# Attention in units of 512 tokens of one sequence and one pair of heads, before a soft mixture of experts

## The chip, the cores and the metric

The kernel runs on one core of one Trainium2 chip, as one launch. The metric is the device time of the launch in microseconds (us), the median of several runs; lower is better. TensorE is called PE, VectorE DVE, ScalarE ACT, GpSimd POOL; SP is the queue of SyncE, from which this kernel issues all its DMAs (transfers between the chip's memory and the core's).

## What is computed

Inputs are q, k and v of shape (8 sequences, 8 heads, 576 tokens, 64), the matrix phi (512 x 32) and the weights w1 (8 experts, 512 x 1024) and w2 (8 experts, 1024 x 512), all float32. First comes attention within chunks of 64 tokens, then a soft mixture of experts over all 4608 tokens with 512 features:

```python
scores = scale * np.matmul(q_c, k_c.transpose(0, 1, 2, 4, 3))   # chunks of 64 tokens, scale = 1/8
scores = scores - np.max(scores, axis=-1, keepdims=True)
attn = np.exp(scores)
attn = attn / (np.sum(attn, axis=-1, keepdims=True) + 1e-09)
out = np.matmul(attn, v_c)
...
logits = x @ phi                       # x: (4608, 512), heads side by side
d = softmax(logits, over tokens);  slot_input = d.T @ x
slot_out[e] = np.maximum(slot_input[e] @ w1[e], 0.0) @ w2[e]     # 4 slots for each of 8 experts
c = softmax(logits, over slots);   return c @ slot_out
```

(The two softmaxes are abridged here; both subtract the maximum and divide by the sum plus 1e-9.)

## The kernel before, in words

**Stages.** The first stage is attention together with the logits, the running maximum and sum over tokens and the running product `d.T @ x`. It goes over 36 units (`NT`). When the last unit is done, the 32 slot inputs are known, and the second stage runs the experts (`up`, `turn`, `down`) and the final product `c @ slot_out` (`combine`), with output transfers at its end.

**A unit before.** The 4608 tokens are taken as one row of 18 groups of 256 tokens (`GT`), regardless of where a sequence ends; a unit is one group and four of the eight heads (`t = 2 g + z`). Since a sequence has 576 tokens, some groups lie across a boundary, and `pieces` (line 127) splits their transfers. `load_qk` (line 136) brings k and q of a unit to SBUF with two tokens of a head in one row of 512 B; `load_v` (line 146) brings v for one tile of 128 tokens with all eight heads, in rows of 256 B. There are eight buffers for q and k (two per unit, so four units deep) and six for v.

**Steps of a unit.** `transposes(t)` (line 150) turns q and k on PE, eight matmuls against the identity (line 156), and four copies bring the result from PSUM to `qkT` in SBUF, three on ACT (line 165) and one on DVE (line 163), de-interleaving even and odd tokens by writes with a stride of two. `s1` (line 169) computes the scores (line 177), their maximum (185) and the difference (187); `s1b` the exponential on ACT (192). `s2a` transposes the result (201, copy 203); `s2b` multiplies with v (219), where a column of ones beside v gives the sums, and normalises into the tile x (228). `s3` transposes x into `xT` (242, copies 247 and 249). Four tiles of 128 tokens make one batch of 512 tokens: `logits`, `weights`, `natural`, `partial`, `combination` run once per batch, that is once in four units.

**Order.** The schedule is written out by hand: in the loop from line 402 on, iteration t issues the loads (`load_qk(t + 5)`, at even t `load_v(t + 2)` and `load_v(t + 3)`, and the weights w1 at an even pace), then `s1(t)`, `transposes(t + 2)`, `s3(t - 3)`, `s2a(t - 1)`, `s1b(t)`, `s2b(t - 2)`, with the steps of a batch between them. The instructions run on each engine in this order. The last two units and the last two batches are unrolled behind the loop (lines 434 to 474). All loads wait in SP's queue in the order in which they are written; a load whose buffer is still being read holds up those behind it.

**End.** `combine(b, h)` (line 602) computes half of the 512 features for batch b and writes 512 rows of 1 KB (line 617): partition p holds four consecutive tokens.

The functions that the change touches:

Of the kernel before, what the change touches and what calls it, by code (L numbers as in the profile page):

```python
# [16 lines left out]
def kernel(  # L17
# [10 lines left out]
    nc = tc.nc  # L28
# [6 lines left out]
    NC = S // CH  # L35
# [4 lines left out]
    GT = 2 * P  # L40
    HZ = H // 2
# [9 lines left out]
    NV = 6  # L51
    NQK = 8

# [18 lines left out]
    qkn = [qk_w[i // 4][:, 512 * (i % 4):512 * (i % 4 + 1)].rearrange("p (h x) -> p h x", h=HZ)  # L72
# [21 lines left out]
    with ExitStack() as actx:  # L94
# [23 lines left out]
        qkT = tiles("qkT", [3, 2, GT], [0])  # L118
        atb = tiles("at", [4, 2, CH], [0])
        sc2 = ap_.tile([P, 2, DM], F32, name="sc2")  # L120
        xb = tiles("x", [2, DM], range(3))
        xT = ap_.tile([P, 4, NF, P], F32, name="xT")
        v_sb = tiles("v", [H, VW], range(NV))
        qkT.update(tiles("qkT", [3, 2, GT], [1]))
        atb.update(tiles("at", [4, 2, CH], [1]))

        def pieces(t0, n):

            o, t = [], t0
            while t < t0 + n:  # L130
                e = min(t0 + n, (t // S + 1) * S)
                o.append((t - t0, e - t, t // S, t % S))
                t = e
            return o

        def load_qk(u):
            g, z = divmod(u, 2)
            for i, src in enumerate((k, q)):
                dst = qkn[(2 * u + i) % NQK]
                for o, n, b, s0 in pieces(GT * g, GT):  # L140
                    nc.sync.dma_start(
                        dst[o // 2:(o + n) // 2],
                        src[b][HZ * z:HZ * (z + 1), s0:s0 + n].rearrange("h (g j) d -> g h (j d)", j=2),
                    )

        def load_v(t):
            for o, n, b, s0 in pieces(P * t, P):
                nc.sync.dma_start(v_sb[t % NV][o:o + n, :, 0:D], v[b][:, s0:s0 + n].rearrange("h x d -> x h d"))

        def transposes(t):  # L150

            pt = pair(f"pqk_{t}")
            for isq in range(2):
                src = qkn[(2 * t + isq) % NQK]
                for h in range(HZ):
                    nc.tensor.transpose(out=pt[:, 1 - isq, P * h:P * (h + 1)], in_=src[:, h], identity=ident)  # L156
            pv = pt.rearrange("x s (hp a g) -> x a s hp g", hp=2, a=2)
            for j in range(2):
                for a in range(2):
                    r = slice(D * a, D * (a + 1))  # L160
                    o = qkT[t % 2][r, 0:2 + a:1 + a].rearrange("x s hp (g j) -> x j s hp g", j=2)[:, j]
                    if j == 1 and (a == 1 or t == 0):
                        nc.vector.tensor_copy(o, pv[D * j:D * (j + 1), a])  # L163
                    else:
                        nc.scalar.copy(o, pv[D * j:D * (j + 1), a])  # L165
# [3 lines left out]
        def s1(t):  # L169
            psc = bank(f"psc_{t}")  # L170
            qT, kb = qkT[t % 2][:, 0], qkT[t % 2][:, 1:3]

            pv = psc.rearrange("p (s a c x) -> p s c a x", s=2, a=2, c=2)
            for c in range(4):
                cs = slice(CH * c, CH * (c + 1))
                for hp in range(2):
                    nc.tensor.matmul(  # L177
                        pv[CH * hp:CH * (hp + 1), c // 2, c % 2],
                        lhsT=qT[:, hp, cs],
                        rhs=kb[:, :, hp, cs],  # L180
                        start=True, stop=True,
                    )
# [11 lines left out]
        xs = {}  # L194
# [11 lines left out]
        def s2b(t):  # L206
            at = ats.pop(t)
            g, z = divmod(t, 2)
            x = xb[g % 3] if g < NT // 2 - 1 else sc2
            rc = a2.tile([P, 2, 4, 1], F32, tag="rc", name=f"rc_{t}")  # L210
            pav = pair(f"pav_{t}")

            for h in range(4):
                for c2 in range(2):
                    for s in range(2):
                        rs = slice(CH * c2, CH * (c2 + 1))
                        nc.tensor.matmul(  # L219
                            pav[CH * s:CH * (s + 1), c2, h * VW:(h + 1) * VW],  # L220
                            lhsT=at[rs, 2 * s + h % 2, h // 2, :],
                            rhs=v_sb[(2 * g + s) % NV][rs, HZ * z + h, :],
                            start=True, stop=True,
                        )
# [3 lines left out]
            nc.vector.tensor_tensor(  # L228
                x[:, :, HZ * D * z:HZ * D * (z + 1)].rearrange("p c (h d) -> p c h d", d=D),
                av[..., 0:D],  # L230
                rc.to_broadcast([P, 2, 4, D]),
                ALU.mult,
            )
            xs[2 * g], xs[2 * g + 1] = x[:, 0], x[:, 1]

        def s3(t):
            px = bank(f"px_{t}")
            g, z = divmod(t, 2)
            for i in range(2):
                for f in range(2):  # L240
                    fs = slice(P * (2 * z + f), P * (2 * z + f + 1))
                    nc.tensor.transpose(  # L242
                        out=px[:, P * (2 * i + f):P * (2 * i + f + 1)], in_=xs[2 * g + i][:, fs], identity=ident)
            pv = px.rearrange("p (s f x) -> p s f x", s=2, f=2)
# [80 lines left out]
        def partial(b):  # L325
            eN, _, al, _ = lst[b]
            pp = bank(f"pp_{b}")
            for j in range(4):
                nc.tensor.matmul(  # L329
                    pp[SL * j:SL * (j + 1), :],  # L330
                    lhsT=eN[:, j, :],
                    rhs=xs.pop(4 * b + j),
                    start=True, stop=True,
                )
# [46 lines left out]
        for t in v_sb.values():  # L381
            nc.gpsimd.memset(t[:, :, D:VW], 1.0)
        load_v(0)
        load_v(1)
# [56 lines left out]
        s2b(t - 3)  # L441
        s2a(t - 1)
# [159 lines left out]
    def combine(b, h):  # L602
# [4 lines left out]
        for j2 in range(2):  # L607
# [9 lines left out]
        nc.sync.dma_start(  # L617
            out[4 * P * b:4 * P * (b + 1), DH * h:DH * (h + 1)].rearrange("(p j) f -> p j f", j=4), ob)
# [58 lines left out]
```

## Time and profile before

| | |
|---|---|
| median of three timed runs | 262.06 us (261.92 to 262.63) |
| time of the profiled execution | 263.49 us |
| its span (first to last instruction) | 261.6 us |
| busy: PE, DVE, ACT, POOL | 223.2, 168.0, 149.7, 7.2 us |
| moved by DMA | 71.86 MB |
| granted PE clock, mean | 0.969 |

In the page of the profile, one digit stands for one fortieth of the span (6.5 us) and gives the busy share in tenths; "DMA" is the mean busy share of the core's 16 DMA engines, as the time of their packets, so overlapping packets can make it exceed 1 in other views. The attention stage goes to about slice 28, the experts and the output to the end. The list of waits gives, for an engine and line, what ended its idle time, the total in us, how often, and the longest. In the list of DMA issues the last number is the median time from issue to landing.

### The profile page before, as it was taken

The numbers are of one execution on the slowest core, as the hardware profiler recorded it, in microseconds if no ns is written. First come the engines' busy times: TensorE is split into PE (matmuls) and PEld (weight loads), VectorE is DVE, ScalarE is ACT, GpSimd is POOL, SyncE is SP. The second block draws the span as 40 slices with busy tenths as digits, with TensorE's granted clock in tenths as the row PEclk, the third lists the DMA queues.
The fourth block names the chain that finished last, engine by engine and source line by source line (L and its number), as shares of the span: only waits on it lengthen the run. The fifth ranks groups of instructions, "written<-read, shape, count | busy, mean of one in ns | idle before, by whom it ended". The sixth has DMA issues, their size and how long they took to land.

```text
span 261.6 us, 7833 instructions
## 1 busy us (share of the span) xinstructions
PE 223.2 (85%) x3205; PEld 164.9 (63%) x3205; DVE 168.0 (64%) x385; ACT 149.7 (57%) x300; POOL 7.2 (3%) x31
## 2 busy tenths in 40 slices
PE   6988988988897988998797697969899999999840
PEld 3666875775785875775684586657563345776840
DVE  4568786886985986986875855867554020755640
ACT  3597857858758758668657366757221220655530
POOL 1000000000000000000000000000004000000000
PEclk9999999999999999999999979999999999999775
DMA  6999599999999999998998995999999999998797
GB/s 181 259 212 228 150 271 245 291 267 254 309 285 262 318 286 259 244 236 267 234 300 232 175 288 136 305 272 343 348 340 339 351 348 348 349 335 272 255 343 250
DMA packets 106962, 71.86 MB, mean 275 GB/s; under 512 B 40368, under 2 KB 102832, under 8 KB 106928
## 3 DMA queue, kind: packets, MB, share of 16 engines
q1 hardware_dynamic: 106928, 71.38, 101.2%
q8 instruction: 25, 0.41, 0.7%
q14 instruction: 9, 0.07, 0.1%
HBM read 61.93 MB, written 9.44 MB: 273 GB/s over the span
## 4 chain that ended last, share of the span: by engine, by line
PE 42%; DMA 23%; DVE 13%; ACT 13%; issue 3%; SPq 2%; ACTq 0%
DMA qk_w<-in_q_dram 23%; ACT qkT L165 10%; PE pf L610 7%; PE po L575 6%; PE ph L545 5%; PE pqk L156 5%; PE px L242 4%; PE psc L177 3%; DVE qkT L163 3%; PE pav L219 3%; DVE x L228 3%; PE pt L201 2%; DVE xT L247 2%; PE pl L259 2%; PE pp L329 2%
## 5 line engine op out<-in xcount | busy, mean ns | idle before, releaser
L165 ACT COPY qkT<-pqk 64x512 f32<-64x512 f32 x107 | 67.0, 626 | 39.7 <-PE pqk L156 37.9
L156 PE MATMUL pqk<-ident,qk_w 128*128 128x128 f32 x288 | 43.9, 291 | 15.4 <-DMA qk_w<-in_k_dram 6.3
L156 PEld LDWEIGHTS pqk<-ident,qk_w 128*128 128x128 f32 x288 | 31.9, 145 | 27.7 <-DVE qkT L163 8.4
L163 DVE COPY qkT<-pqk 64x512 f32<-64x512 f32 x37 | 25.8, 698 | 32.4 <-ACT qkT L165 29.7
L177 PE MATMUL psc<-qkT 128*64 128x128 f32 x576 | 40.2, 282 | 0.3 <-DVE qkT L163 0.3
L177 PEld LDWEIGHTS psc<-qkT 128*64 128x64 f32 x576 | 31.4, 138 | 3.7 <-issue 1.2
L219 PE MATMUL pav<-v,at 64*64 64x65 f32 x1152 | 25.8, 227 | 0.9 <-issue 0.6
L187 DVE TENSOR_TENSOR sc<-psc,mx 128x512 f32<-128x512 f32 x36 | 24.9, 691 | 1.3
L242 PE MATMUL px<-ident,x 128*128 128x128 f32 x136 | 21.8, 284 | 4.3 <-DVE x L228 4.1
L219 PEld LDWEIGHTS pav<-v,at 64*64 64x64 f32 x1152 | 20.7, 136 | 7.0 <-issue 5.9
L185 DVE TENSOR_REDUCE mx<-psc 128x8 f32<-128x512 f32 x36 | 24.4, 677 | 0.3 <-PE psc L177 0.2
L228 DVE TENSOR_TENSOR x<-pav,rc 128x512 f32<-128x512 f32 x34 | 23.5, 691 | 1.2
L201 PE MATMUL pt<-ident,sc 128*128 128x128 f32 x144 | 22.3, 279 | 1.8 <-ACT sc L192 1.8
L242 PEld LDWEIGHTS px<-ident,x 128*128 128x128 f32 x136 | 15.4, 143 | 12.7 <-DVE x L228 10.9
L192 ACT ACTIVATE sc<-sc 128x512 f32<-128x512 f32 x36 | 23.0, 639 | 0.3 <-DVE sc L187 0.3
L203 ACT COPY at<-pt 128x512 f32<-128x512 f32 x36 | 21.2, 589 | 1.9 <-PE pt L201 1.5
L610 PE MATMUL pf<-sst,cst 128*128 128x256 f32 x72 | 18.7, 413 | 0.9 <-DVE sst L597 0.9
L201 PEld LDWEIGHTS pt<-ident,sc 128*128 128x128 f32 x144 | 17.0, 143 | 2.7 <-ACT sc L192 2.5
L610 PEld LDWEIGHTS pf<-sst,cst 128*128 128x128 f32 x72 | 17.4, 329 | 1.9 <-DVE sst L597 1.3
L616 DVE COPY ob<-pf 128x512 f32<-128x512 f32 x18 | 12.2, 689 | 4.1 <-PE pf L610 4.0
L545 PE MATMUL ph<-w,siT 128*32 128x512 f32 x128 | 14.4, 594 | 0.3 <-DVE s_rd L375 0.3
L614 ACT COPY ob<-pf 128x512 f32<-128x512 f32 x18 | 10.5, 586 | 7.0 <-PE pf L610 6.8
(95 smaller groups left out, 203.4 us busy)
## 6 DMA issues: line engine op xcount, KB each, us to landing
w<-in_moe_w_dram SPq DMA_DIRECT2D x30, 1024.0 KB, 8.4
out_dram<-ob SPq DMA_DIRECT2D x18, 512.0 KB, 5.1
v<-in_v_dram SPq DMA_DIRECT2D x32, 256.0 KB, 6.6
qk_w<-in_k_dram SPq DMA_DIRECT2D x24, 256.0 KB, 6.6
qk_w<-in_q_dram SPq DMA_DIRECT2D x24, 256.0 KB, 6.5
qk_w<-in_moe_w_dram SPq DMA_DIRECT2D x2, 1024.0 KB, 10.3
qk_w<-in_k_dram SPq DMA_DIRECT2D x8, 192.0 KB, 5.7
qk_w<-in_q_dram SPq DMA_DIRECT2D x8, 192.0 KB, 5.8
```

The source lines that it names most:

```text
L156: nc.tensor.transpose(out=pt[:, 1 - isq, P * h:P * (h + 1)], in_=src[:, h], identity=ident)
L163: nc.vector.tensor_copy(o, pv[D * j:D * (j + 1), a])
L165: nc.scalar.copy(o, pv[D * j:D * (j + 1), a])
L177: nc.tensor.matmul(pv[CH * hp:CH * (hp + 1), c // 2, c % 2], lhsT=qT[:, hp, cs], rhs=kb[:, :, hp, cs], start=True, stop=True,)
L185: nc.vector.reduce_max(mx, pv, axis=AX.X)
L187: nc.vector.tensor_tensor(sc.rearrange("p (r x) -> p r x", x=CH), pv, mx.unsqueeze(2).to_broadcast([P, 8, CH]), ALU.subtract)
L201: nc.tensor.transpose(out=pt[:, P * r:P * (r + 1)], in_=sc[:, r], identity=ident)
L219: nc.tensor.matmul(pav[CH * s:CH * (s + 1), c2, h * VW:(h + 1) * VW], lhsT=at[rs, 2 * s + h % 2, h // 2, :], rhs=v_sb[(2 * g + s) % NV][rs ...
L228: nc.vector.tensor_tensor(x[:, :, HZ * D * z:HZ * D * (z + 1)].rearrange("p c (h d) -> p c h d", d=D), av[..., 0:D], rc.to_broadcast([P, 2 ...
L242: nc.tensor.transpose(out=px[:, P * (2 * i + f):P * (2 * i + f + 1)], in_=xs[2 * g + i][:, fs], identity=ident)
L545: nc.tensor.matmul(ph[SL * i:SL * (i + 1), :], lhsT=siT[:, j, :], rhs=wt[1, e, j // 2][:, j % 2, DM * h:DM * (h + 1)], start=(j == 0), sto ...
L610: nc.tensor.matmul(pf[:, DH * j:DH * (j + 1)], lhsT=cv[:, 2 * j2 + j, :], rhs=sst[h], start=True, stop=True)
```

## The change

A unit is now 512 tokens of one sequence (the first 512 of its 576) and a pair of heads; four units (`NHP`) make a batch of 512 tokens with all heads, and there are eight such batches. The last 64 tokens of all eight sequences together are a ninth batch, which is computed fifth. So no load crosses a sequence's end, and `pieces` is gone.

- q and k come with four tokens in a row of 1 KB; each unit has two such loads of 256 KB, or four of 128 KB in the batch of the last tokens. Because four tokens lie side by side, the eight transposes now take two 128-column blocks per head, and the copies of lines 163 and 165 read PSUM alternating between two blocks (`g i`), and write with a stride of two as before.
- v comes per unit, in rows of 256 B as before, in two transfers (one per head), four in the batch of last tokens; it has four buffers, one per unit, and `load_v(t + 1)` is issued in every iteration. `load_v(35)` is issued behind the loop, after `s2b(32)` is written and behind the second load of w2 into `qk_w`.
- `s1`, `s2b`, `s3` and `partial` use other indices; the numbers and shapes of their instructions stay. x has two buffers of a whole batch. `s3` fills one block of 128 features for all four lanes, where it filled two blocks for two lanes.
- Outputs go to their sequence's rows; the batch of the last tokens writes each half in four transfers, one for each of the four consecutive tokens of a partition.

The core of the diff:

```diff
-    GT = 2 * P
-    HZ = H // 2
+    BT = 4 * P
+    RT = S - BT
+    JT = 4
+    GT = RT // JT
-    NV = 6
+    NV = 4
+    batch = [0, 1, 2, 3, B] + list(range(4, B))
...
         def load_qk(u):
-            g, z = divmod(u, 2)
+            n, hp = divmod(u, NHP)
+            hs = slice(2 * hp, 2 * hp + 2)
             for i, src in enumerate((k, q)):
                 dst = qkn[(2 * u + i) % NQK]
-                for o, n, b, s0 in pieces(GT * g, GT):
+                if batch[n] < B:
+                    nc.sync.dma_start(dst, src[batch[n], hs, 0:BT].rearrange("a (g j) d -> g a (j d)", j=JT))
+                else:
+                    for a in range(2):
+                        nc.sync.dma_start(
+                            dst[:, a], src[:, 2 * hp + a, BT:S].rearrange("b (g j) d -> g b (j d)", j=JT))
...
+        def load_v(u):
+            n, hp = divmod(u, NHP)
+            hs = slice(2 * hp, 2 * hp + 2)
+            dst = v_sb[u % NV][..., 0:D]
+            if batch[n] < B:
+                for a in range(2):
                     nc.sync.dma_start(
+                        dst[:, :, a], v[batch[n], 2 * hp + a, 0:BT].rearrange("(r x) d -> x r d", x=P))
+            else:
+                for c2 in range(2):
+                    for a in range(2):
+                        nc.sync.dma_start(dst[CH * c2:CH * (c2 + 1), :, a],
+                                          v[c2::2, 2 * hp + a, BT:S].rearrange("r x d -> x r d"))
...
-            pv = pt.rearrange("x s (hp a g) -> x a s hp g", hp=2, a=2)
+            if batch[u // NHP] < B:
+                pv = pt.rearrange("x s (a i g) -> x a s g i", a=2, i=2)
+                dv = dst.rearrange("x s (g i j) -> x j s g i", i=2, j=2)
+            else:
+                pv = pt.rearrange("x s (a i g b) -> x a s b g i", a=2, i=2, b=B)
+                dv = dst.rearrange("x s (b g i j) -> x j s b g i", b=B, i=2, j=2)
...
-            o = xT[:, 2 * (g % 2):2 * (g % 2) + 2, 2 * z:2 * z + 2]
+            o = xT[:, :, hp]
...
-            if t % 2 == 0:
-                load_v(t + 2)
-                load_v(t + 3)
+            load_v(t + 1)
...
         s2b(t - 3)
+        load_v(t)
         s2a(t - 1)
...
-        nc.sync.dma_start(
-            out[4 * P * b:4 * P * (b + 1), DH * h:DH * (h + 1)].rearrange("(p j) f -> p j f", j=4), ob)
+        ov = out.rearrange("(b s) f -> b s f", s=S)[..., DH * h:DH * (h + 1)]
+        if batch[b] < B:
+            nc.sync.dma_start(ov[batch[b], 0:BT].rearrange("(p j) f -> p j f", j=4), ob)
+        else:
+            for j in range(4):
+                nc.sync.dma_start(ov[:, BT + j:S:4], ob[:, j])
```

More of the change, by code (lines that the diff above doesn't have):

```diff
@@ L34 @@
     CH = 64
-    NC = S // CH
+    NHP = H // 2
     DM = H * D
@@ L71 @@
     qk_w = [const.tile([P, 2048], F32, name=f"qk_w{i}") for i in range(2)]
-    qkn = [qk_w[i // 4][:, 512 * (i % 4):512 * (i % 4 + 1)].rearrange("p (h x) -> p h x", h=HZ)
+    qkn = [qk_w[i // 4][:, 512 * (i % 4):512 * (i % 4 + 1)].rearrange("p (a x) -> p a x", a=2)
            for i in range(NQK)]
@@ L125 @@
+        qkT.update(tiles("qkT", [3, BT], [1]))
         atb.update(tiles("at", [4, 2, CH], [1]))
[L127 to L134, printed above, removed]
         def load_qk(u):
-            g, z = divmod(u, 2)
+            n, hp = divmod(u, NHP)
+            hs = slice(2 * hp, 2 * hp + 2)
             for i, src in enumerate((k, q)):
@@ L139, in load_qk @@
                 dst = qkn[(2 * u + i) % NQK]
-                for o, n, b, s0 in pieces(GT * g, GT):
[L141 to L148, printed above, removed]
@@ new lines, in transposes @@
+        def transposes(u):
+            pt = pair(f"pqk_{u}")
+            for isq in range(2):
+                src = qkn[(2 * u + isq) % NQK]
+                for a in range(2):
+                    for i in range(2):
+                        o = P * (2 * a + i)
+                        nc.tensor.transpose(
+                            out=pt[:, 1 - isq, o:o + P], in_=src[:, a, P * i:P * (i + 1)], identity=ident)
+            dst = qkT[u % 2]
+            if batch[u // NHP] < B:
[4 more added lines that the diff above has]
+                dv = dst.rearrange("x s (b g i j) -> x j s b g i", b=B, i=2, j=2)
@@ L158, in transposes @@
             for j in range(2):
                 for a in range(2):
-                    r = slice(D * a, D * (a + 1))
-                    o = qkT[t % 2][r, 0:2 + a:1 + a].rearrange("x s hp (g j) -> x j s hp g", j=2)[:, j]
-                    if j == 1 and (a == 1 or t == 0):
+                    o = dv[D * a:D * (a + 1), j, 0:2 + a:1 + a]
+                    if j == 1 and (a == 1 or u == 0):
                         nc.vector.tensor_copy(o, pv[D * j:D * (j + 1), a])
@@ L171, in s1 @@
             qT, kb = qkT[t % 2][:, 0], qkT[t % 2][:, 1:3]
[L173 to L182, printed above, removed]
+            pv = psc.rearrange("p (m a c x) -> p m c a x", m=2, a=2, c=2)
+            for c in range(8):
+                m, c2, r2 = c // 4, c // 2 % 2, c % 2
+                o = P * (2 * m + r2) + CH * c2
+                nc.tensor.matmul(
+                    pv[CH * r2:CH * (r2 + 1), m, c2],
+                    lhsT=qT[:, o:o + CH],
+                    rhs=kb[:, :, o:o + CH],
+                    start=True, stop=True,
+                )
             pv = psc.rearrange("p (r x) -> p r x", x=CH)
@@ L233, in s2b @@
             )
-            xs[2 * g], xs[2 * g + 1] = x[:, 0], x[:, 1]
         def s3(t):
             px = bank(f"px_{t}")
[L238 to L244, printed above, removed]
-            o = xT[:, 2 * (g % 2):2 * (g % 2) + 2, 2 * z:2 * z + 2]
+            n, hp = divmod(t, NHP)
+            for j in range(4):
+                nc.tensor.transpose(
+                    out=px[:, P * j:P * (j + 1)], in_=xb[n % 2][:, j % 2, hp, j // 2], identity=ident)
+            pv = px.rearrange("p (j x) -> p j x", j=4)
+            o = xT[:, :, hp]
             if t == NT - 1 or t % 2 == 0 and t < NT - 6:
@@ L381 @@
         for t in v_sb.values():
-            nc.gpsimd.memset(t[:, :, D:VW], 1.0)
+            nc.gpsimd.memset(t[..., D:VW], 1.0)
         load_v(0)
-        load_v(1)
         for t in qkT.values():
```

32 lines of the change are left out of this document (13 added, 19 removed).

## The prediction

> **What bounds the kernel now.** I read the page first, then the list of waits, then windows cut at the starts of every fourth unit, then the DMA view and single rows of SP.
>
> ```profile
> span 261.6 us, 7833 instructions
> ...
> DMA  6999599999999999998998995999999999998797
> GB/s 181 259 212 228 150 271 245 291 267 254 309 285 262 318 286 259 244 236 267 234 300 232 175 288 136 305 272 343 348 340 339 351 348 348 349 335 272 255 343 250
> ...
> PE 42%; DMA 23%; DVE 13%; ACT 13%; issue 3%; SPq 2%; ACTq 0%
> ```
>
> ```profile
> PE pqk L156 <- DMA qk_w<-in_k_dram: 6.3, 8, 1.9
> ...
> PE pqk L156 <- DMA qk_w<-in_q_dram: 1.7, 6, 0.4
> ```
>
> The DMA engines are busy in almost every slice, but they move about 250 GB/s in the first 27 slices (attention) and 348 in the slices behind (weights of the second product). In attention, then, a busy engine moves less. The chain gives 23% to loads of q; that counts each load from its issue, so it tells where the end hangs on transfers, not what would be saved. What would be saved is in the waits: PE sat 6.3 + 1.7 = 8.0 us before line 156, the transposes, with k or q not there. That is the ceiling of what faster loads can give.
>
> The bounds below are starts of line 177 in units 8, 12, ..., 32; each block is four units with the same work (the first and the last of these starts from the PE timeline, then the windows: length, busy time of PE, PEld, DVE, ACT, POOL, granted clock, DMA share, GB/s).
>
> ```profile
> 40.53 1.09 PE L177 MATMUL psc<-qkT 128*64 128x128 f32 x16
> ...
> 163.37 1.09 PE L177 MATMUL psc<-qkT 128*64 128x128 f32 x16
> ```
>
> ```profile
> 40.53:60.20 19.67, 17.34 (x304) 13.74 (x299) 15.55 (x35) 13.74 (x29) 0.40 (x1) 1.00 1.07 268
> 60.20:80.25 20.05, 17.58 (x305) 13.75 (x299) 15.61 (x35) 14.04 (x29) 0.40 (x1) 1.00 1.09 282
> 80.25:99.33 19.08, 17.37 (x304) 13.76 (x298) 15.62 (x35) 14.01 (x29) 0.40 (x1) 1.00 1.16 285
> 99.33:118.72 19.39, 17.83 (x306) 13.86 (x299) 15.61 (x35) 14.02 (x29) 0.40 (x1) 1.00 1.05 239
> 118.72:139.68 20.96, 17.42 (x304) 13.76 (x299) 15.62 (x35) 13.99 (x29) 0.40 (x1) 1.00 1.07 264
> 139.68:163.37 23.69, 18.75 (x305) 15.03 (x299) 15.63 (x35) 14.76 (x30) 0.40 (x1) 0.93 0.89 211
> ```
>
> The third block, 19.08 us, is what the four compute engines need when the data is there (PE busy 17.37, DVE 15.62, ACT 14.01, and the hand-overs between them). Six blocks take 122.84 us, six times the best one 114.48: 8.36 us are lost. The granted clock of 0.93 in the last block accounts for 0.07 x 23.69 = 1.66 us. The other 6.7 us fit the waits on k and q; the remaining 1.3 us of the 8.0 lie before unit 8 and after unit 32.
>
> **The change, part by part.**
>
> *Rows of q and k (lines 136 to 144).* The first rows are the first and the last of the four groups of issues of k (24 + 8 + 8 + 8 = 48; q has the same); behind them stand, for a stretch with nearly only 512 B rows and one with nearly only 1 KB rows, the packets and the window.
>
> ```profile
> qk_w<-in_k_dram SPq DMA_DIRECT2D x24, 256.0 KB, 6.6
> ...
> qk_w<-in_k_dram SPq DMA_DIRECT2D x8, 64.0 KB, 5.6
> ```
>
> ```profile
> DMA packets 1193, 0.59 MB, mean 295 GB/s; under 512 B 40, under 2 KB 1193, under 8 KB 1193
> ```
>
> ```profile
> DMA packets 5164, 5.22 MB, mean 348 GB/s; under 512 B 80, under 2 KB 5163, under 8 KB 5163
> ```
>
> ```profile
> 10.00:12.00 2.00, 1.64 (x18) 1.02 (x14) 1.71 (x3) 0.22 (x2) 0.00 (x0) 1.00 1.18 295
> ```
>
> ```profile
> 205.00:220.00 15.00, 14.57 (x185) 6.59 (x177) 1.71 (x9) 2.11 (x4) 0.00 (x0) 1.00 1.09 348
> ```
>
> k and q have 8 x 8 x 576 x 64 elements of 4 B each, together 18.9 MB. Between 10 and 12 us the packets are 0.59 MB / 1193 = 495 B on average, nearly all rows of 512 B of q and k, and move at 295 GB/s with the engines full; between 205 and 220 us they are 1 KB rows (second-layer weights), at 348. 18.9 MB take 64.0 us by the first and 54.2 us by the second: 9.8 us of transfer time less, or 1.1 us per block of four units (2.1 MB). The mean loss on transfers per block is 6.7 / 6 = 1.1 us. The relief is thus about as large as the waits, and because a late transfer delays the next ones, small reliefs count fully once the queue stops falling behind. I take 6.5 of the 8.0 us: 5.5 in the blocks, 1.0 at the two ends. Bounds: 0 (the waits have another cause, first rival) and 8.0.
>
> [...]
>
> *v (lines 146 to 148).* The issues of v and of the outputs before, then two rows of SP:
>
> ```profile
> v<-in_v_dram SPq DMA_DIRECT2D x32, 256.0 KB, 6.6
> ...
> v<-in_v_dram SPq DMA_DIRECT2D x8, 128.0 KB, 7.5
> ```
>
> ```profile
> out_dram<-ob SPq DMA_DIRECT2D x18, 512.0 KB, 5.1
> ```
>
> ```profile
> 163.27 0.46 SPq L141 DMA_DIRECT2D qk_w<-in_q_dram  x1
> 163.82 6.11 SPq L148 DMA_DIRECT2D v<-in_v_dram  x2
> ```
>
> Same bytes, same rows of 256 B, hence the same transfer time; but two issues per unit (four for the last tokens), 80 instead of 40. q and k go from 96 issues to 80, outputs from 18 to 24. In all 30 issues more, on SP, at about 0.46 us each (the first of the SP rows): 14 us of SP spread over 260, beside everything else. The wait of `load_v(t + 1)` for the buffer of unit t - 3 ends when that unit's line 219 is through, at the end of iteration t - 1; behind it on SP stand the weights and the next q and k, whose buffers come free only in the middle of iteration t. So it holds nothing up: 0, at the most 6.1 us once, as in the second SP row, if SP is late anyhow. The new last load, `load_v(35)`, stands behind two weight loads of 1 MB (3 us each at 348 GB/s) that are released by the last transposes.
>
> ```profile
> 173.86 1.09 PE L177 MATMUL psc<-qkT 128*64 128x128 f32 x16
> ```
>
> ```profile
> 184.41 0.69 PE L219 MATMUL pav<-v,at 64*64 64x65 f32 x29 [0.57 <-issue]
> ```
>
> Released about when unit 34 starts (173.86), it has 10 us until unit 35 reads it (184.41), and lands some 6.6 to 7.5 us later, as v's loads do: 0, and up to 2 us if the queue is one load longer.
>
> *Copies out of PSUM (lines 163, 165).* Same elements, same stride-2 writes; but the reads now alternate between two 128-column blocks instead of running along one. Rows that bear on a strided read: a DVE reduction from PSUM with a stride of 32 (line 348), one from SBUF with stride 32 (388), one without (320), and the copies of q and k themselves.
>
> ```profile
> L348 DVE TENSOR_REDUCE mm<-pr x1: 279/279/279, 191.5 to 191.5; 1x32 f32<-1x128 f32 x1
> ```
>
> ```profile
> L388 DVE TENSOR_REDUCE sel<-ident x1: 375/375/375, 3.9 to 3.9; 128x32 f32<-128x128 f32 x1
> ```
>
> ```profile
> L320 DVE TENSOR_REDUCE cs<-c_all x9: 270/274/286, 48.6 to 197.2; 128x4 f32<-128x128 f32 x9
> ```
>
> ```profile
> L165 ACT COPY qkT<-pqk 64x512 f32<-64x512 f32 x107 | 67.0, 626 | 39.7 <-PE pqk L156 37.9
> ```
>
> From PSUM the stride costs nothing (279 against 274 ns), from SBUF 101 ns for 128 elements. The source here is PSUM, so I take 0; the upper bound, by the SBUF row, is 512 / 128 x 101 = 0.40 us a copy (second rival). ACT with such a source is not in the trace.
>
> *Matmuls, x, xT.* The same number of transposes and products of the same shapes, with contiguous runs of 64 or 128 columns; x has two buffers of four units in place of three of two units, and `partial(n - 2)` comes two iterations before the first write of batch n: 0. In the tail, the last unit brings one feature block instead of the last lanes, so three quarters of the last `logits` need not wait for it: 0 to -0.5, taken as 0.
>
> *Outputs of the last tokens (line 617).* The end is a drain of output transfers. The last copy of a result starts at 251.50, and the DMA engines stay full behind it:
>
> ```profile
> 251.50 0.69 DVE L616 COPY ob<-pf 128x512 f32<-128x512 f32 x1 [0.24 <-PE pf L610]
> ```
>
> ```profile
> out_dram<-ob SPq DMA_DIRECT2D x9, 512.0 KB, 5.5
> ```
>
> ```profile
> 250.00:255.00 5.00, 1.46 (x7) 1.26 (x6) 1.71 (x3) 1.17 (x2) 0.00 (x0) 0.72 1.04 343
> ```
>
> 512 KB at 343 GB/s are 1.5 us, so nine of them are a queue of 13.8 us. Batch 4 of the changed kernel writes its 512 KB in four transfers with an outermost extent of 8 in place of one with 512 rows. If the engines share these evenly, nothing changes; if only half of them carry it, that piece takes 3.0 us, and the full queue passes on 1.5 us. I take 1.5, since nothing hides unevenness in a full queue; bounds 0 and 1.5, and below zero nothing, as bytes and rows are the same. (The earlier half, h = 0, is written while PE is the chain: 0.)
>
> [...]
>
> **Sum.** -6.5 (waits on q and k) + 0 (v) + 0 (copies) + 0 (matmuls) + 1.5 (outputs), and -0.5 for the four loads of the first two units, which stand before all work and take 0.9 us each at 295 and 0.75 at 348 GB/s (256 KB): -5.5 us. The profiled execution had a span of 261.6 and a time of 263.49; the median of the timed runs is 262.06, so I subtract from that: 256.6 us. A difference of 0.3%, 0.8 us, is what a measurement can tell here.
>
> **Rivals.** (1) *The transfers are late because they are issued late, not because the engines are full.* For it: in the worst block the DMA share is 0.89 and only 211 GB/s move, while PE waits; and SP stood 6.1 us in two loads of v. Against it: the other five blocks have shares of 1.05 and more, and late issues follow when the queue does not drain. Then the wider rows give nothing: 262.1, or 263.6 with the outputs. (2) *ACT pays for the strided read* (slower). The place is line 165, three copies a unit, 108 in all, on the way from transposes to scores. At 0.40 us each a block's ACT time goes from 14.0 to 18.8 us and the blocks lengthen by up to 4.8 us; over nine blocks 43 us, about 300 us. It decides from 5.5 / 108 = 51 ns a copy on. Against it: line 348. [...]
>
> **How the numbers follow.** Forecast 0.75; rival 1 0.12 (a third of it still gains a little from fewer pieces, the rest is split by the outputs' cost); rival 2 0.08; rival 3 0.05. Range: all waits gone, no cost for outputs, start 1 us earlier: 262.1 - 9.0 = 253.1, and a little below since the best block may itself hold a wait: 252.5. Upwards, a third of the waits gone and the outputs' 1.5 is 261; I go to 261.5, which leaves out rival 2 and most of 1 and 3. Faster 0.78, same 0.08, slower 0.14.
>
> **What would show it.** PE's wait for k and q at the transposes falls from 8.0 us to about 1.5; blocks of four units take 19 to 19.5 us; packets fall by some 18,000; DMA's GB/s in attention rises in spite of the same share; the copies of line 165 stay at 626 ns; between the last copy and the end lie 1.5 us more. Wrong: copies above 680 ns; blocks above 20 us with PE still waiting for q or k (then rival 1, if DMA's share is below 0.95); or waits on v at line 219, of which there are none now.

## The result and the profile after

The changed kernel takes 253.15 us (median of 4 runs, 251.27 to 255.08); the kernel before, on the same chip, 262.35 (261.92 to 264.62). The ratio is 0.961 (95% interval 0.952 to 0.970). Two later comparisons gave 0.970 (0.966 to 0.975) and 0.968 (0.963 to 0.974), with the changed kernel at 252.6 and 253.5 us. The forecast was 256.6 (252.5 to 261.5): the direction held, but the gain of some 9 us is 60% more than the 5.5 of the sum. By the first ratio 262.06 us become 251.8, just below the range; by the two others 254.3 and 253.7.

The profile that came with the result is of a disturbed execution, so the rows below are those of the same kernel run again (e1: time 252.66 us). First the page: DMA in tenths, GB/s, packets, the chain by engine and the groups of the copies out of PSUM.

```profile
span 250.5 us, 7897 instructions
...
DMA  6999999999989899999999888992499999999987
GB/s 185 331 296 269 302 322 248 321 292 209 283 176 301 218 327 247 304 333 313 333 336 323 206 282 239 295 304 63 157 345 348 348 348 347 348 374 335 341 262 265
DMA packets 88947, 71.87 MB, mean 287 GB/s; under 512 B 40784, under 2 KB 84816, under 8 KB 88912
...
PE 49%; DVE 24%; ACT 16%; issue 4%; DMA 2%; SPq 0%; ACTq 0%; DVEq 0%
...
L181 ACT COPY qkT<-pqk 64x512 f32<-64x512 f32 x107 | 66.6, 622 | 30.2 <-PE pqk L166 28.5
...
L179 DVE COPY qkT<-pqk 64x512 f32<-64x512 f32 x37 | 25.9, 699 | 22.6 <-ACT qkT L181 19.3
```

Transfers have 2% of the chain now, where loads of q alone had 23% before. The copies take what they took (622 ns on ACT against 626). Next the waits of PE, and the blocks of four units as in the prediction (windows between the starts of the scores of units 8, 12, ..., 32; the clock, DMA's share and GB/s stand last):

```profile
PE pqk L166 <- DMA qk_w<-in_k_dram: 0.7, 2, 0.5
```

```profile
41.36:59.44 18.08, 17.34 (x304) 13.77 (x299) 15.57 (x35) 12.99 (x28) 0.40 (x1) 1.00 1.00 284
59.44:78.47 19.03, 17.33 (x304) 13.77 (x299) 15.61 (x35) 13.97 (x29) 0.40 (x1) 1.00 0.92 247
...
116.54:135.57 19.03, 17.33 (x304) 13.76 (x299) 15.61 (x35) 13.97 (x29) 0.40 (x1) 1.00 1.12 325
135.57:154.61 19.04, 17.34 (x305) 13.77 (x299) 15.61 (x35) 13.97 (x29) 0.40 (x1) 1.00 0.89 256
```

From the second block on every block takes 19.03 or 19.04 us: the pace of the compute engines. DMA's share goes from 0.89 to 1.12 without an effect on the blocks, and the clock is 1.00 throughout. Two rows more for an account of the span: the first product of the experts, and the last copy of a result; of before the same two rows are 196.54 (below) and 251.50 (in the prediction).

```profile
185.16 7.07 PE L555 MATMUL ph<-w,siT 128*32 128x512 f32 x64
...
239.32 0.69 DVE L626 COPY ob<-pf 128x512 f32<-128x512 f32 x1 [0.24 <-PE pf L620]
```

```profile
196.54 1.92 PE L545 MATMUL ph<-w,siT 128*32 128x512 f32 x16 [0.25 <-DVE s_rd L375]
```

| stretch | before, us | after (e1), us | difference |
|---|---|---|---|
| start to the scores of unit 8 | 40.53 | 41.36 | +0.83 |
| unit 8 to unit 32 | 122.84 | 113.25 | -9.59 |
| unit 32 to the first product of the experts | 33.17 | 30.55 | -2.62 |
| from there to the last copy | 54.96 | 54.16 | -0.80 |
| last copy to the end | 10.05 | 11.16 | +1.11 |
| span | 261.55 | 250.48 | -11.07 |

A third profile of the changed kernel (e12, span 250.6) gives -0.16, -8.92, -2.62, -0.31 and +1.05. So the gain is made in the blocks and in the tail of attention, and the end gives one microsecond back. The stages add up to more than the medians show: the profile of before took 263.49 us and that of e1 252.66, a difference of 10.8, where the medians differ by 8.7 to 9.2.

### The profile page after: what moved, and what is told of

Read it like the earlier page. It is cut to its first block, busy times and chain, and to the rows that moved or that the text cites. A ratio compares the mean times of both kernels' runs of the same rounds, so it can differ in the third digit from the quotient of the medians.

```text
span 252.9 us, 7897 instructions
## 1 busy us (share of the span) xinstructions
PE 220.7 (87%) x3205; PEld 164.3 (65%) x3205; DVE 167.9 (66%) x385; ACT 149.3 (59%) x300; POOL 7.1 (3%) x29
## 4 chain that ended last, share of the span: by engine, by line
PE 49%; DVE 24%; ACT 16%; issue 4%; DMA 2%; SPq 0%; ACTq 0%; DVEq 0%
ACT qkT L181 13%; PE pf L620 7%; PE pqk L166 7%; PE psc L193 6%; PE po L585 6%; PE ph L555 6%; DVE qkT L179 6%; DVE x L243 5%; PE pav L234 4%; PE px L254 4%; PE pt L216 3%; DVE xT L259 2%; DVE mx L201 2%; PE pl L271 2%; DMA qk_w<-in_k_dram 2%
## 5 line engine op out<-in xcount | busy, mean ns | idle before, releaser
L166 PE MATMUL pqk<-ident,qk_w 128*128 128x128 f32 x288 | 42.0, 292 | 6.1 <-DVE qkT L179 5.3
L166 PEld LDWEIGHTS pqk<-ident,qk_w 128*128 128x128 f32 x288 | 32.8, 147 | 15.3 <-DVE qkT L179 8.7
L254 PE MATMUL px<-ident,x 128*128 128x128 f32 x144 | 22.8, 282 | 7.1 <-DVE x L243 6.5
L243 DVE TENSOR_TENSOR x<-pav,rc 128x512 f32<-128x512 f32 x36 | 24.9, 691 | 1.2
L216 PE MATMUL pt<-ident,sc 128*128 128x128 f32 x144 | 21.9, 275 | 1.5 <-ACT sc L208 1.5
L626 DVE COPY ob<-pf 128x512 f32<-128x512 f32 x18 | 12.2, 690 | 4.0 <-PE pf L620 4.0
```

The lines of the kernel that those rows point to most:

```text
L166: nc.tensor.transpose(out=pt[:, 1 - isq, o:o + P], in_=src[:, a, P * i:P * (i + 1)], identity=ident)
L216: nc.tensor.transpose(out=pt[:, P * r:P * (r + 1)], in_=sc[:, r], identity=ident)
L243: nc.vector.tensor_tensor(xb[n % 2][:, :, hp].rearrange("p c m (a d) -> p c (m a) d", a=2), av[..., 0:D], rc.to_broadcast([P, 2, 4, D]), A ...
L254: nc.tensor.transpose(out=px[:, P * j:P * (j + 1)], in_=xb[n % 2][:, j % 2, hp, j // 2], identity=ident)
```

## The experiments

They had to settle three questions: what of the loads costs before (the width of rows, the splitting, or both), what happens when there are many small loads, and what the outputs of the last tokens cost. Ratios are to the kernel before on the same chip.

**e1, e12: the changed kernel again.** No edit.

> The changed kernel once more, for a second profile and its time on the same chip as the next three. Both theories: 251 to 254 us, blocks of four units at 19.05 us, the granted clock 1.00 through attention (if the dip to 0.93 in the profile of before was a chance event of that execution).

> The kernel after, unchanged, as the measure for e10 and e11 on this chip: ratio 0.96 to 0.975, drain 11 to 12 us.

Measured: 252.61 us, 0.970 (0.966 to 0.975), and 253.54 us, 0.968 (0.963 to 0.974).

**e8: the kernel before again.** No edit, one execution.

> The kernel before once more, for a second profile. If the dip of the granted clock to 0.93 in the last block was a chance event, this one has no such dip, a last block of 21 to 22 us and a time of about 262 us; if it belongs to the kernel, it is there again.

Measured: span 263.2 us; the blocks take 21.07, 18.96, 19.32, 21.22, 20.68 and 22.69 us. The same 9 us or so are lost as in the first profile, but in other blocks: the loads are late by a little nearly everywhere, and no single place is to blame. The granted clock is 0.92 in the first and in the last of these blocks and 1.00 in the others, so the dip of the first profile comes with this kernel.

**e3, e4: the changed kernel with each load of q and k in two.** e4 splits by heads and keeps rows of 1 KB; e3 splits the rows and so makes them 512 B. Both have the same number of loads (144).

```diff
-                    nc.sync.dma_start(dst, src[batch[n], hs, 0:BT].rearrange("a (g j) d -> g a (j d)", j=JT))
+                    for a in range(2):      # e4
+                        nc.sync.dma_start(
+                            dst[:, a], src[batch[n], 2 * hp + a, 0:BT].rearrange("(g j) d -> g (j d)", j=JT))
+                    for y in range(2):      # e3
+                        nc.sync.dma_start(
+                            dst[:, :, P * y:P * (y + 1)],
+                            src[batch[n], hs, 0:BT].rearrange("a (g j) d -> g a (j d)", j=JT)[:, :, P * y:P * (y + 1)])
```

> The changed kernel with rows of 512 B again: each load of q and k (of the 32 units within a sequence) split in two transfers that carry half of every row. Theory (the width of the rows made the gain): waits on q and k return, blocks lengthen to 19.5 to 21 us, 258 to 262 us. Rival (the gain comes from units that do not cross a sequence's end and from the order of the loads): 252 to 254 us.

> The control for the run with half rows: each load of q and k split in two transfers as well, one per head, with rows of 1 KB kept. Theory (width of the rows): as the changed kernel, 251 to 254 us. Rival (the number of transfers matters, not their rows): as the run with half rows.

Measured: e3 269.66 us, 1.032 (1.026 to 1.038); e4 263.33 us, 1.010 (1.005 to 1.015). The row width makes 6.3 us of difference, but the larger part, 10.7 us against the changed kernel, is lost by splitting alone. Neither expectation of e4 holds: it lies between the changed kernel and e3. Of e4, first two blocks, then three of the waits of SP's queue:

```profile
76.66:97.03 20.37, 17.73 (x305) 13.72 (x298) 15.60 (x35) 14.02 (x29) 0.40 (x1) 1.00 0.74 205
97.03:120.61 23.58, 19.60 (x305) 14.38 (x299) 15.69 (x35) 14.05 (x29) 0.40 (x1) 0.93 0.90 268
```

```profile
SPq L139 <- DMA w<-in_moe_w_dram: 11.0, 8, 1.7
...
SPq L143 <- DMA w<-in_moe_w_dram: 5.0, 2, 2.6
SPq L157 <- DMA w<-in_moe_w_dram: 4.9, 3, 2.4
```

The DMA engines have time left (0.74) while PE waits. In e4's numbering lines 139, 143 and 157 are loads of q, k and v (143 and 157 those of the last tokens). They have nothing to do with w1, yet SP holds them 20.9 us in these three rows until a load of w1 has landed. The traces of before and after show the tie: SP's transfers (187 and 217) name eight semaphores in turn, counters that rise as a transfer lands, and each transfer from the ninth on stands behind a wait for its own semaphore. In before none of these 179 was issued until the one eight places ahead had landed. Eight whole loads of q and k are 2 MB, eight halves 1 MB, so less can be under way, most of all behind a load of 1 MB that has to land first.

**e5, e6, e7: the kernel before with lighter loads.** e5 loads q and k as 512 tokens by two heads in rows of 1 KB (so not those of the unit); e6 keeps rows of 512 B but no load crosses a sequence's end (so some units have other tokens); e7 leaves out the loads of v after the first six tiles.

```diff
+                nc.sync.dma_start(                                            # e5
+                    dst.rearrange("p (a y) x -> p a (y x)", a=2),
+                    src[min(n, B - 1), 2 * hp:2 * hp + 2, 0:4 * P].rearrange("a (g j) d -> g a (j d)", j=4))
+                b, s0 = g // 2 % B, GT * (g % 2)                              # e6
+                nc.sync.dma_start(
+                    dst, src[b][HZ * z:HZ * (z + 1), s0:s0 + GT].rearrange("h (g j) d -> g h (j d)", j=2))
         def load_v(t):
+            if t >= NV:                                                       # e7
+                return
```

> The kernel before with the loads of q and k alone changed: each brings 512 tokens of two heads of one sequence in rows of 1 KB, as many bytes as before, one transfer each for q and k. The rest of the program takes them for 256 tokens of four heads, so q and k are not those of the unit. Theory (width of the rows): most of the gain, 253 to 256 us, blocks at 19.1 us. Rival (the gain comes from v, x and the order): 260 to 263 us.

> The kernel before with rows of 512 B, but each load of q and k taken from inside one sequence, so that none is split at a sequence's end (64 issues fewer... 72 in place of 96); some units read the wrong tokens. Theory (width of the rows): 259 to 262 us, blocks still above 19.5 us on average. Rival (splits at sequence ends cause the late loads): 253 to 256 us.

> The kernel before without the loads of v behind the first six tiles (7.9 MB of transfers left out; later units multiply with the old v). It shows what the kernel before gains when the DMA engines are relieved in another way. Theory (engines full of small rows make the loads late): all waits on q and k go, blocks at 19.1 us, 251 to 254 us. Rival (loads are late because they are issued late): above 258 us.

Measured: e5 250.96 us, 0.958 (0.950 to 0.966); e6 252.87 us, 0.964 (0.953 to 0.974); e7 251.70 us, 0.961 (0.954 to 0.969). Each of them alone brings the blocks to 19.0 to 19.1 us, e6 with rows of 512 B; so the theory that e6 was expected to bear out, that the width alone does it, fails there. Two blocks of e6:

```profile
78.19:97.26 19.07, 17.36 (x306) 13.76 (x298) 15.61 (x35) 14.02 (x29) 0.40 (x1) 1.00 1.10 316
135.40:154.49 19.09, 17.38 (x305) 13.77 (x299) 15.62 (x35) 14.03 (x29) 0.40 (x1) 1.00 1.01 245
```

Three different reliefs with one result: that speaks for a resource that they share and that is just short before. e7 alone would not show it, since it also takes v's waits for free buffers out of SP's queue; e5 and e6 keep them. The blocks of e7 from unit 12 on have shares of only 0.68 to 0.86 and still take 19.05 to 19.07 us, so faster loads cannot make a block shorter than this. e6 changed two things against before: 24 loads fewer, and no pieces that cover only 32, 64 or 96 partitions.

**e9, e10: w1 from another queue.** The loads of w1 in attention are issued from POOL and have a queue of their own (q0 below); SP's waits no longer name them (every row of e10, every row of e9 from 0.8 us on). A copy of one element holds each to its old place in time. e9 is the kernel before with that, e10 is e4 with it.

```diff
+        dma = nc.sync.dma_start
+        if first is not None:
+            nc.gpsimd.tensor_copy(t[0:1, 0:1], first)
+            dma = nc.gpsimd.dma_start
...
-                load_w(wpa, nw)
+                load_w(wpa, nw, qkT[(t + 1) % 2][0:1, 0, 0, 0:1])
```

> The kernel before, with the sixteen loads of w1 in the attention stage (1 MB each) issued from POOL's queue in place of SP's, each behind a copy of one element that holds it to the same place in the order. In the compiled program SP's transfers use eight semaphores in turn, so that a transfer waits for the one eight places before it to land; the transfers of POOL have semaphores of their own. Theory R (too few bytes may be under way: a load of q, k or v stands in SP's queue until the transfer eight places ahead has landed, longest when that is 1 MB of w1, and a load that a sequence's end has split takes several of the eight places): the loads stand no longer behind w1, blocks of four units take 19.0 to 19.3 us and the time is 252 to 256 (ratio 0.96 to 0.98), with rows of 512 B and all 96 loads of q and k kept. Theory S (SP's own time per issue, about 0.5 us): 16 issues of some 150 are gone, under 1 us: ratio 0.995 to 1.0. Theory T (every transfer costs the DMA engines a fixed time, wherever it is issued): ratio 1.0.

> The kernel of e4 (after, each load of q and k as two of 1 KB rows, 1.01 of the time before) with the loads of w1 in attention issued from POOL's queue. R: the small loads wait no longer for w1 to land, most of what e4 gave back returns: ratio 0.965 to 0.985, waits of SP on w gone from 20.9 us. S and T: the same number of loads of q, k and v at the same price, ratio 1.0 to 1.01.

Measured: e9 263.53 us, 1.005 (1.000 to 1.010): what theory R expected of the kernel before does not come. w1 was not much in the way there, and SP waits more for its own loads of k instead. First a row of before, then one of e9:

```profile
SPq L141 <- DMA w<-in_moe_w_dram: 3.7, 2, 2.5
```

```profile
SPq L152 <- DMA qk_w<-in_k_dram: 8.2, 4, 3.6
```

In attention SP's waits for landings are 6.0 us in all before and 10.4 in e9. So e9 takes w1 out of the limit of eight, but not the limit away.

e10 260.22 us, 0.984 (0.973 to 0.995): it brings back some six tenths of what e4 had given up against the changed kernel (1.010 to 0.984, with 0.968 for that kernel in the same comparison; four to nine tenths by e10's interval), at the upper end of what R expected. Its profile is of an execution of 256.16 us. The stretch from unit 32 to the experts is 30.54 us there as in the changed kernel, where e4 had 38.57, but one block still takes 22.88 us, and SP now waits for its own small loads to land, 19.7 us in seven rows of which these are the largest:

```profile
SPq L156 <- DMA qk_w<-in_q_dram: 5.9, 6, 1.6
SPq L143 <- DMA qk_w<-in_k_dram: 4.9, 3, 2.2
```

What made the one block late stays open. Of e9 a block with a long wait and one that runs well:

```profile
43.67:68.38 24.71, 19.49 (x303) 15.95 (x298) 15.05 (x35) 12.55 (x26) 1.45 (x4) 0.86 1.05 248
106.34:125.45 19.11, 17.39 (x305) 13.77 (x299) 15.62 (x35) 14.02 (x29) 2.17 (x5) 1.00 1.18 262
```

The engines are full in both (1.05 and 1.18): w1 from another queue takes nothing off them.

These two runs also show what each kind of transfer costs the DMA engines, since w1 now has a queue of its own (q0). In e9 between 22 and 155 us: packets, MB, share of the 16 engines' time.

```profile
q1 hardware_dynamic: 54813, 20.23, 75.7%
q0 software_dynamic: 3536, 13.63, 30.0%
```

w1 takes 2.20% of that stretch per MB (2.09% in e10); q, k and v take 3.74%. With the rate of 2.20% for w1 the other kernels can be divided too. Before, e6, e13, e14, e5 and after (e1), all between 22 and 155 us; in them 13, 14, 14, 13, 15 and 15 loads of w1 of 1.05 MB were issued:

```profile
q1 hardware_dynamic: 58563, 33.74, 103.8%
```

```profile
q1 hardware_dynamic: 61314, 35.48, 103.4%
```

```profile
q1 hardware_dynamic: 61422, 34.97, 102.0%
```

```profile
q1 hardware_dynamic: 47149, 34.62, 99.7%
```

```profile
q1 hardware_dynamic: 50330, 38.16, 102.1%
```

```profile
q1 hardware_dynamic: 49072, 37.22, 99.2%
```

For before: 33.74 - 13 x 1.05 = 20.1 MB in 103.8 - 30.0 = 73.8%, that is 0.2725 MB per per cent. A load of w1 counted too many or too few at the edge of the stretch would shift an entry by 0.004 to 0.006. Other executions and kernels agree: e8 gives 0.27 as before does, e12 0.33 as e1 does, and e4, whose engines are not full (91.2%), 0.34 where e3 with the same number of loads has 0.30. This estimate for the rest, beside the ratios:

| kernel | rows of q and k | loads of q and k that are split | MB of q, k, v per per cent | ratio |
|---|---|---|---|---|
| before | 512 B | 24, by partitions | 0.27 | 1 |
| e6 | 512 B | none | 0.29 | 0.964 |
| e13 | 512 B | 24, by heads | 0.29 | 0.977 |
| e14 | 1 KB | 24, by partitions | 0.30 | 0.973 |
| e5 | 1 KB | none | 0.33 | 0.958 |
| after (e1) | 1 KB | the last tokens', by heads | 0.33 | 0.970 |

**e13, e14: width and splitting apart.** e13 is e6 with the 24 loads split by heads, two pieces of 128 partitions each; e14 is e5 with them split by partitions, as before.

```diff
+                m = HZ // len(pieces(GT * g, GT))                             # e13
+                for h in range(0, HZ, m):
+                    nc.sync.dma_start(
+                        dst[:, h:h + m],
+                        src[b][HZ * z + h:HZ * z + h + m, s0:s0 + GT].rearrange("h (g j) d -> g h (j d)", j=2))
+                for o, w, _, _ in pieces(GT * g, GT):                         # e14
+                    r = slice(o // 2, (o + w) // 2)
+                    nc.sync.dma_start(
+                        dst[r].rearrange("p (a y) x -> p a (y x)", a=2),
+                        src[min(n, B - 1), 2 * hp:2 * hp + 2, 0:4 * P].rearrange("a (g j) d -> g a (j d)", j=4)[r])
```

> The kernel of e6 (rows of 512 B, no load crosses a sequence's end, some units with other tokens than the reference's), but the 24 loads of q and k that are split before are split here too, by heads: two pieces of 128 partitions each instead of 32 with 96 or 64 with 64. 96 loads of q and k as before. Theory N (pieces on few partitions cost the DMA engines time; by the shares of the engines between 22 and 155 us, w1 taken at 2.2% a MB, q, k and v come at 0.27 MB per per cent before, 0.29 in e6, 0.33 after): 0.29 MB per per cent, blocks 19.0 to 19.3 us, ratio 0.96 to 0.97. Theory C (the number of loads, by SP's issues or by waits for the transfer eight places ahead): the gain of e6 is gone, ratio 0.99 to 1.0.

> The kernel of e5 (rows of 1 KB, q and k not the unit's own), but the loads that are split before are split here too, at the same partitions (32 with 96, 64 with 64). 96 loads of q and k as before, in rows of 1 KB. Theory E (the DMA engines' time is what ends last before; wide rows and whole loads each save enough of it): 0.30 MB per per cent, blocks 19.0 to 19.3 us, ratio 0.96 to 0.975. Theories N alone and C: splitting is all that matters, ratio 0.99 to 1.0.

Measured: e13 254.63 us, 0.977 (0.969 to 0.985), all blocks of units 8 to 32 at 18.8 to 19.1 us; e14 254.76 us, 0.973 (0.965 to 0.981), blocks 19.1 to 20.5 us, three of them above the 19.3 that were expected. The engines' time came out at the 0.29 and 0.30 MB per per cent that were expected, and the gain did not vanish in either, as the opposite theories had it; the ratio of e13 is a little above the range. So 24 loads more cost the engines nothing that shows (0.29 in e13 and e6), pieces on few partitions cost 7 to 10% (0.27 before against 0.29 in e13, 0.30 in e14 against 0.33 in e5), and rows of 512 B 10 to 14% (0.27 before against 0.30 in e14, 0.29 in e6 against 0.33 in e5, 0.30 in e3 against 0.34 in e4). Either relief brings most of the gain. What e13 gives up against e6 lies between unit 32 and the experts (34.72 against 32.60 us), what e14 gives up against e5 mostly in its blocks; both have 24 loads more in the same queue. Of e14 a wait of PE and one of SP:

```profile
PE pqk L157 <- DMA qk_w<-in_k_dram: 3.7, 6, 1.5
```

```profile
SPq L143 <- DMA w<-in_moe_w_dram: 6.3, 2, 4.0
```

In attention SP waits 8.7 us for landings in e14, 1.9 in e13 and not at all in e5 and e6. (The profile of e14 is of an execution of 257.62 us, 2.9 above its median.)

**e2, e11: the outputs of the last tokens.** e2 writes each half as eight transfers, one per sequence, 16 partitions each. e11 keeps four transfers, but the lanes of that batch are stored in another order, so that the outermost extent on both sides is 16 or a multiple of it (`B` is 8).

```diff
+                for s in range(B):                                            # e2
+                    nc.sync.dma_start(ov[s, BT:S].rearrange("(p j) f -> p j f", j=4), ob[16 * s:16 * (s + 1)])
+            for j in range(4):                                                # e11
+                nc.sync.dma_start(ov[:, BT + j:S:4].rearrange("s g f -> g s f"), ob[:, j])
...
+            if batch[b] == B:                                                 # e11, in place_c
+                for c in range(2):
+                    nc.scalar.copy(
+                        cs[0:PH].rearrange("r (g j s c i) -> r j c s g i", j=2, s=2, c=2, i=4)[:, j, c],
+                        pc[PH * j:PH * (j + 1), P * c:P * (c + 1)].rearrange("r (s g i) -> r s g i", s=2, i=4))
+                continue
```

> The changed kernel with the outputs of the last tokens as eight transfers (one per sequence, 16 partitions, outermost extent 16) in place of four (outermost extent 8). Theory: the four transfers use half of the engines and hold up the full queue behind the last result, so this is 1.5 to 2.2 us faster than the changed kernel, and the stretch at 140 GB/s after the last copy is gone. Rival (the queue drains at its own rate): within 0.5 us of the changed kernel.

> The kernel after, with the last tokens' lanes in another order (line 523's copies for that batch, four instead of two), so that their outputs go in four transfers whose outermost extent is 16 in place of 8. By the drain of after (half of the engines busy for 3 us, 11.2 to 12.3 us between the last copy and the end against 10.0 before): all 16 engines carry them, the drain is 10 us again, and the time 1 to 2 us below the kernel after on this chip. Rival: e2's 2.8 us were lost with transfers that use 16 engines too, so the cost is that of small transfers in the drain and this kernel takes what after takes.

Measured: e2 255.38 us, 0.979 (0.975 to 0.983), 2.8 us slower than the changed kernel on its chip; the drain behind the last copy is 14.5 us. Neither expectation of e2 holds. e11 250.69 us, 0.959 (0.953 to 0.964), 2.9 us faster than the changed kernel on its chip (e12), with a drain of 10.1 us against 11.1. The three drains from the last copy on (e1, e2, e11), each as a window; share and GB/s stand last:

```profile
239.32:250.48 11.16, 0.00 (x0) 0.00 (x0) 0.69 (x1) 0.12 (x1) 0.00 (x0) 0.54 0.79 254
```

```profile
238.35:252.80 14.45, 0.00 (x0) 0.00 (x0) 0.69 (x1) 0.11 (x1) 0.00 (x0) 0.62 0.85 249
```

```profile
238.03:248.10 10.07, 0.00 (x0) 0.00 (x0) 0.69 (x1) 0.11 (x1) 0.00 (x0) 0.68 0.88 281
```

and the middle of e1's and e2's, in forty slices of e1's drain and in one window of e2's:

```profile
DMA  9997455555679999999999999999999999200000
GB/s 340 289 132 92 73 154 165 190 187 183 219 219 311 355 351 369 362 377 362 366 340 373 373 362 369 340 373 358 348 351 351 347 347 300 88 15 0 0 0 0
```

```profile
241.70:245.00 3.30, 0.00 (x0) 0.00 (x0) 0.00 (x0) 0.00 (x0) 0.00 (x0) 0.50 0.72 128
```

In the changed kernel the engines are at about five tenths for some 2 us, as when half of them have nothing to do; with the extent of 16 the drain's share rises from 0.79 to 0.88 and its length falls to what it was before (10.05). In e2 the engines are at seven tenths and still move only 128 GB/s: busy, and slow. e11 is the fastest version of the change. Of the 2.4 us between its profile and e12's, 1.0 is in the drain, 0.9 before unit 8 (39.50 against 40.37 us, a stretch that varies between executions of one kernel) and 0.5 between the first product of the experts and the last copy; only the first microsecond is shown to come from the edit.

## Where the prediction was right, and which step failed

**Rows of q and k: the right mechanism, sized too small.** The prediction took 6.5 us of waits of 8.0 and called the 8.0 "the ceiling of what faster loads can give". That step failed. Blocks and tail together gained 11.5 to 12.2 us by the profiles (8.92 or 9.59, and 2.62), and by the medians about 10 (8.7 to 9.2, and the 1.1 that the outputs took back): the term that was taken as -6.5 came to -10 or more, beyond the 8.0 either way. Three things were left out:

- The sum by blocks, 8.36 us, stood beside it and was the better measure, but 1.66 us of it were put to the clock as if the clock were a cost of its own. It is not shown to be one: in before, e1, e4, e5, e6, e8, e9, e10 and e12 the blocks that take 19.1 us or less have a clock of 1.00, and it is lower only in long blocks or right behind one (0.93 in the last block of before and in a block of e4, 0.86 in a block of e9). It came back with the loads. That the waits lower it is argued from this, not shown.
- The list of waits put some of the loads' time to others. Two waits of PE at the transposes are named after `xT` and `cs`, but end with the landing of a load of k (issued at 34.47 and landed at 42.66, and at 170.83); with them the waits on loads are 8.0 + 1.18 + 1.09 = 10.3 us, 9.1 of them from unit 8 on. (Of the 8.0, 6.3 lie in the blocks and 1.7 outside, where the prediction had 6.7 and 1.3.) In before's PE timeline:

```profile
42.80 1.40 PE L156 MATMUL pqk<-ident,qk_w 128*128 128x128 f32 x8 [1.18 <-DVE xT L247]
...
170.97 0.63 PE L156 MATMUL pqk<-ident,qk_w 128*128 128x128 f32 x4 [1.09 <-DVE cs L320]
```

- The stretch from unit 32 to the experts lost about 2.4 us to late loads, where the prediction had 1.0 for both ends. e5 shows it: with no more than the loads of q and k changed, the stretch takes 30.80 us against 33.17 before and 30.55 in e1.

**Why wider rows helped so surely.** The prediction compared 295 with 348 GB/s, 1.1 us of transfer time per block. By the engines' shares the relief is larger: q, k and v of four units are 3.15 MB, which take 3.15 / 0.2725 = 11.6% of 133 us, 15.4 us, before and 12.6 us after; w1 takes 6.5 us in both (2.13 loads per block). That makes 21.9 us before and 19.1 after, for a block of 19.05 us: 1.15 and 1.00 of it. The highest share that any block shows is 1.18, in e9, so by this estimate before had next to no time left. The estimate does not rank the kernels by itself: e6 and e13 with 1.10 run at pace, e14 with 1.07 does not quite. SP's waits for landings, which are long in e14, may be the reason; it is not shown. Of the 2.8 us that the change saves, 1.5 come with the rows (15.4 against 13.9 in e14) and 1.3 (1.1 by e6 against before) with what the prediction did not price at all: the change also removes the loads' pieces on 32, 64 and 96 partitions. It named the fewer pieces only as a small gain under the first rival.

What few partitions cost shows in two places: e2's transfers on 16 partitions move 128 GB/s at a share of 0.72 with several under way, and loads with pieces on 32, 64 and 96 partitions cost the engines 7 to 10% more over all of q, k and v. No run here has a single transfer on 32 or 64 partitions by itself, and why such pieces cost more is not shown.

**Rival 3, that 512 B is enough.** By it the wider rows would gain nothing; its chance of 0.05 was the author's estimate. As a statement on the engines it fails: on 128 partitions the engines bring 14% more in the same time with rows of 1 KB (0.33 against 0.29). As a statement on the time it holds for another change: with whole loads and rows of 512 B PE waits only 0.5 us for q and k in all (e6; 1.5 in e5). The 1.9 us by which e6 is slower than e5 lie almost all behind unit 32 (32.60 against 30.80 us), 1.5 of them in an idle time of PE for which the profile names no cause.

**Rival 1, loads late because they are issued late.** It is not what limits the kernel before. e13 shows it better than e9, which did not take the limit of eight away: with the same 96 loads in the same queue and rows of 512 B, pieces on 128 partitions alone bring the blocks to pace. It becomes the limit as soon as there are many small loads (e4, DMA's share 0.74 while PE waits; e10 takes some six tenths of it away). The change goes some way towards it, with v in 64 loads of 128 KB, and does not reach it.

**Rival 2, the strided read on ACT.** It does not occur: 622 ns a copy on ACT against 626. The reduction with a stride from PSUM (279 against 274 ns) was the right row to go by.

**Outputs of the last tokens.** Predicted +1.5, measured +1.1 (e1) and +1.05 (e12), and e11 takes it back. That half of the engines carry these transfers was the author's estimate, since no view of before has one of this form; the drains agree with it: e1's engines are at about five tenths for some 2 us, and the share over the drain rises from 0.79 to 0.88 in e11.

**The other terms.** v: 0, and no wait for v at line 234. First loads: -0.5 was taken, +0.8 and -0.2 measured, so nothing that can be told. Matmuls, x and xT: 0 in the blocks, and of the 2.6 us of the tail at most some 0.25 (30.80 in e5, which keeps them as before, against 30.55). The packets fell by 18,015, as said.

## What to carry to other kernels

When several transfers share a stretch, add up what each kind costs the DMA engines (share per MB from the table of queues) and hold the sum against the pace of the compute engines; a kernel that stands just above it can gain nearly the whole lateness from a small relief (e5, e6 and e7 each did here), and the waits that the profile puts down to loads need not be the ceiling of that gain (here 8.0 us of waits and about 10 of gain). Price a load by the partitions it covers (7 to 10% of the engines' time here) as well as by its row (10 to 14%), and split by another axis than partitions where it must be split. Fewer bytes per transfer are no relief by themselves: a queue that lets only so many transfers be under way, eight in this program, can starve behind one large load (e4: 20.9 us of SP's waits, and a share of 0.74 in a block where PE waits).

## What the runs showed of the hardware beyond expectation

- Pieces of a load on 32 to 96 partitions cost the DMA engines 7 to 10% over all of q, k and v although only a third of the loads of q and k had them; eight transfers of 16 partitions moved 128 GB/s at a share of 0.72, where before's outputs of 512 KB move 343 at 1.04 (250 to 255 us).
- The shares of the engines can stand above 1 for a whole block (1.18 in e9), so a share of 1.00 is not yet a full queue.
- The granted clock was 1.00 in every block of before, e1, e4, e5, e6, e8, e9, e10 and e12 that took 19.1 us or less. In their other blocks it fell only with long waits (0.93 in 23.69 us before, 0.86 in 24.71 in e9) or right behind one (0.92 in 19.63 us in e10, behind 22.88), and not in all of them (1.00 in 21.22 us in e8).
